# Tables of reciprocals with five rows for each head, and three read-backs in place of seven

## The chip, the core and the metric

The kernel runs on one core of a Trainium2 chip. Five engines work side by side: TensorE (PE in the profile, its weight loads PEld), VectorE (DVE), ScalarE (ACT), GpSimd (POOL) and SyncE (SP), which here only issues transfers. Sixteen DMA engines move data between DRAM and the on-chip memories. The metric is the device time of one execution in microseconds.

## What is computed

Two linear-attention blocks (A and B) work on the same input of 2048 tokens by 640 features and are mixed by a gate. Each has 32 heads of 20 features.

```python
q, k, v = qkv[0], qkv[1], qkv[2]
phi = lambda t: jnp.where(t > 0, t + 1, jnp.exp(t)) + 1e-6
pq, pk = phi(q), phi(k)
kv = jnp.einsum("bhsd,bhse->bhde", pk, v)
z = jnp.einsum("bhsd->bhd", pk)
num = jnp.einsum("bhqd,bhde->bhqe", pq, kv)
den = jnp.einsum("bhqd,bhd->bhq", pq, z)[..., None] + 1e-6
o = num / den
... @ wo
g = _sigmoid((x * gate_w).sum(-1, keepdims=True))
return g * a + (1 - g) * b
```

The division has one denominator for each head and token. It can be moved ahead: the query features `pq` of a head are multiplied by 1/den of that head before the last matmul.

## The kernel before

Everything is bf16 with f32 sums. `XT` holds the transposed input, `PK[X]` the key features of branch X by token (16 tiles of 128), `PQ[X]` the query features with features on the partitions: five tiles `k` of 128 features by 2048 tokens, worked in four blocks `b` of 512 tokens. Tiles 0 and 1 hold the even and the odd features of the first 256 in turn, tiles 2 and 3 those of the next 256, and tile 4 the last 128. So in the first pair partition p holds features of head p // 10, in the second those of head (128 + p) // 10, and in tile 4 that of head (512 + p) // 20.

The order of the engines' work is written out by hand: a list of operations, each with what it reads and writes, from which a small scheduler (`_Sched`) derives the semaphore waits. Each engine does its operations in the order of that list. A transfer is issued by SyncE in its own order, and its waits stand in SyncE's queue ahead of it, so a transfer whose data isn't ready holds up all that stand behind it.

The stages: keys of both branches (`k_tile`), queries (`q_tile`) with branch A's products `x^T pk` (`g_piece`) between them, then branch B's products, then for each branch the combined weights `WP` (`m_part`, `wp_tile`), and the final tiles: `fin_mm(X, t)` multiplies 128 tokens of `PQ[X]` with `WP[X]`; ScalarE scales branch A's by the gate (`fin_a`, line 793), VectorE adds branch B's (`fin_out`, line 805), and the tile is stored.

Around the change, all within `wp_a_den` (line 885), which is put on the list just after the second of branch B's 20 pieces: `den` (line 637) puts the denominators of one branch into one bank of 128 partitions, where partition 32 b + h holds head h of block b and the columns are the block's 512 tokens. VectorE adds the small constant (line 652) and takes reciprocals in four quarters of 128 columns (line 660) into `RC[X]`. `table(X)` (line 672) writes `RC[X]` to the DRAM tensor `rs[X]` of 32 rows (heads) by 2048 columns (tokens). `widen(X, b0, b1)` (line 682) reads it back into `RXW[X]`, where each partition has the reciprocals of its own head; there are three groups `i`, for the two pairs and for tile 4. Since 128 isn't a multiple of 10 or 20, a group begins or ends within a head, and the list `runs` (line 666) has seven transfers for the three groups: (group, first partition, first head, heads, partitions per head). Block 0 of A, block 0 of B, blocks 1 to 3 of A and blocks 1 to 3 of B are read back in this order, 28 transfers.

`scale(X, b)` (line 694) multiplies block b of `PQ[X]`: one VectorE instruction for the four tiles of the two pairs (line 699), one for tile 4 (line 707). On the list `scale("A", 0)` stands among branch B's products; `scale("B", 0)` behind final tiles A0 and A1, `scale("A", 1)` behind `WP` of branch B, just ahead of `fin_mm("A", 3)`, and the other five between output tiles. Tile t reads block t // 4: A4 is the first to need A's block 1.

`RXW["A"]` lies over the first ten tiles of `PK["A"]`, and `RXW["B"]` over three chunks of `XT`; the keys in `RX_LAP` stand for the memory that they share. All transfers go through `dma` (line 283), so a transfer is L291 in the profile, and all matmuls through `mms`, L302.

Of the kernel before, what the change touches and what calls it, by code (L numbers as in the profile page):

```python
# [7 lines left out]
dt = mybir.dt  # L8
# [3 lines left out]
S = 2048  # L12
D = 640
H = 32
DH = 20
NT = 16
NB = 4
# [188 lines left out]
def bass_gated_mix__linear_attn_block__linear_attn_block__prompt_kernel(  # L206
# [10 lines left out]
    consts = nc.inline_tensor(_build_consts(), name="kconsts")  # L217
    cap = consts.ap().bitcast(dt.bfloat16)

    rs = {X: nc.dram_tensor("rs" + X, [H, S], dt.bfloat16).ap() for X in ("A", "B")}  # L220
    wqkv = {"A": A_wqkv, "B": B_wqkv}
    wo = {"A": A_wo, "B": B_wo}
    BR = ("A", "B")
# [1 line left out]
    with ExitStack() as es:  # L225
        E = es.enter_context

        def sb(name, shape, dtype=dt.bfloat16):
            return E(nc.sbuf_tensor(name, shape, dtype))
# [16 lines left out]
        RXW = {  # L246
            "A": PK["A"][:, 0:10, :].rearrange("p t f -> p (t f)")[:, 0 : 3 * S].rearrange("p (i n) -> p i n", i=3),
            "B": XT[:, 0:3, :],
        }
        RX_LAP = {  # L250
            "A": [("PK", "A", t) for t in range(10)],
            "B": [("XT", t, c) for t in range(NT) for c in range(3)],
        }
# [12 lines left out]
        RC = {X: sb("RC" + X, [128, 512]) for X in BR}  # L266
# [16 lines left out]
        def dma(eng, name, o_ap, i_ap, reads=(), writes=(), transpose=False, noncontig=None):  # L283
            sem = new_sem(name)

            def fn(engobj):
                if noncontig is not None:
                    with nc.allow_non_contiguous_dma(reason=noncontig):
                        ins = engobj.dma_start(o_ap, i_ap, transpose=transpose)
                else:  # L290
                    ins = engobj.dma_start(o_ap, i_ap, transpose=transpose)  # L291
                return ins.then_inc(sem, 16)

            return sch.op(eng, fn, reads=reads, writes=writes, name=name, sem=sem, total=16)
# [19 lines left out]
        def dve(fn, reads=(), writes=(), name=""):  # L314
            return sch.op("DVE", fn, reads=reads, writes=writes, name=name)
# [33 lines left out]
        def load_wk(eng, X, c0, c1):  # L349
# [19 lines left out]
            reads=[("ONE",)],  # L369
            writes=[("IDN",)],  # L370
# [3 lines left out]
            writes=[("SGE", 0)],  # L374
# [7 lines left out]
        for b in range(1, NB):  # L382
            for c in range(NC):
# [5 lines left out]
                    writes=[("XT", t, c) for t in range(4 * b, 4 * b + 4)],  # L389
# [247 lines left out]
        def den(X, bk):  # L637
            xi = BR.index(X)
            steps = []
            for k in range(NC):  # L640
                for b in range(NB):
                    o = bank(bk, 0, 512, 32 * b, 32 * b + 32)
                    r = PQ[X][:, k, 512 * b : 512 * b + 512]
                    steps.append((o, ZBD[:, NC * xi + k, :], r, k == 0, k == NC - 1, (0, 32 * b)))
            mms(
                steps,
                reads=[("ZBD", X)] + [("PQ", X, b, k) for k in range(NC) for b in range(NB)],
                writes=[("PS", bk)],
                name="den%s" % X,
            )  # L650
            dve(
                lambda e: e.tensor_scalar(DT32[X][:, :], bank(bk, 0, 512), EPS, None, op0=ALU.add),  # L652
                reads=[("PS", bk)],
                writes=[("DT", X)],
            )

        def recip(X, i):
            def rcp(e):
                with nc.allow_low_precision(reason="r goes into a bf16 matmul"):
                    return e.reciprocal(RC[X][:, 128 * i : 128 * i + 128], DT32[X][:, 128 * i : 128 * i + 128])  # L660

            dve(rcp, reads=[("DT", X)], writes=[("RC", X, i)])

        runs = (
# [3 lines left out]
        )  # L670

        def table(X):
            dma(
                "SP",
                "rs" + X,
                rs[X].rearrange("h (b n) -> b h n", b=NB),
                RC[X][:, :],
                reads=[("RC", X, j) for j in range(4)],
                writes=[("RS", X)] + RX_LAP[X],
            )  # L680

        def widen(X, b0, b1):
            for n, (i, p0, h0, nh, m) in enumerate(runs):
                c0, c1 = 512 * b0, 512 * b1
                dma(
                    "SP",
                    "rx%s%d%d" % (X, b0, n),
                    RXW[X][p0 : p0 + nh * m, i, c0:c1],
                    rs[X][h0 : h0 + nh, c0:c1].unsqueeze(1).to_broadcast([nh, m, c1 - c0]),
                    reads=[("RS", X)],  # L690
                    writes=[("RX", X, i, p0, b) for b in range(b0, b1)],
                )

        def scale(X, b):
            cols = slice(512 * b, 512 * b + 512)
            pairs = RXW[X][:, 0:2, cols]
            v = PQ[X][:, 0:4, cols].rearrange("p (i a) n -> p i a n", i=2)
            dve(
                lambda e: e.tensor_tensor(
                    out=v, in0=v, in1=pairs.unsqueeze(2).to_broadcast([128, 2, 2, 512]), op=ALU.mult  # L700
                ),
                reads=[("RX", X) + r[0:2] + (b,) for r in runs if r[0] < 2] + RX_LAP[X],
                writes=[("PQ", X, b, k) for k in range(4)],
            )
            v4 = PQ[X][:, 4, cols]
            dve(
                lambda e: e.tensor_tensor(out=v4, in0=v4, in1=RXW[X][:, 2, cols], op=ALU.mult),  # L707
                reads=[("RX", X) + r[0:2] + (b,) for r in runs if r[0] == 2] + RX_LAP[X],
                writes=[("PQ", X, b, 4)],
            )  # L710

# [27 lines left out]
        def wp_tile(X, k, pp):  # L739
            P = PP[pp]  # L740
            cells = []
            for g in range(4):
                w = 8 + g // 2 if k == 4 else 4 * (k // 2) + g
                fs = slice(32 * (g % 2), 32 * (g % 2) + 32) if k == 4 else slice(k % 2, 64, 2)
                cells.append((w, MG[:, w, fs]))
            for j, (lo, hi) in enumerate(((0, D // 2), (D // 2, D))):
                mms(
                    [
                        (P[32 * g : 32 * g + 32, 512 * j : 512 * j + hi - lo], l, wo_at(X, w)[0][:, lo:hi], True, True, (0, 32 * g))
                        for g, (w, l) in enumerate(cells)  # L750
                    ],
                    reads=[("WO", X, w) for w, _ in cells] + [("MG", w) for w, _ in cells],
                    writes=[("PS", 2 * pp + j)],
                    name="wp%s%d" % (X, k),
                )
            for j, (lo, hi) in enumerate(((0, D // 2), (D // 2, D))):
                o, p = WP[X][:, k, lo:hi], P[:, 512 * j : 512 * j + hi - lo]
                (dve if j else act)(
                    lambda e, o=o, p=p, j=j: e.tensor_copy(o, p) if j else e.activation(o, p, ACT.Copy),
                    reads=[("PS", 2 * pp + j)],  # L760
                    writes=[("WP", X, k, j)],
                )
# [96 lines left out]
        for i in range(8):  # L859
            n = 3 * i + 9  # L860
# [24 lines left out]
        def wp_a_den():  # L885
            for k in range(NC):
                wp_tile("A", k, (1, 2, 3)[k % 3])
            den("A", 6)
            den("B", 7)
            for X in BR:  # L890
                for i in range(4):
                    recip(X, i)
                table(X)
            for b0, b1 in ((0, 1), (1, NB)):
                for X in BR:
                    widen(X, b0, b1)
# [4 lines left out]
            _Chain(nA, [(0, lambda: z_turn("B", 7))]),  # L901
            _Chain(nA, [(0, lambda: [m_part("A", 0, 8, 2), m_part("A", 8, NW, 3)])]),
            _Chain(nA + 1, [(0, wp_a_den), (15, lambda: scale("A", 0))]),
        ]
        _interleave(mains, chains)
        for t in (0, 1):
            fin_mm("A", t)
            fin_a(t)
        scale("B", 0)
        m_part("B", 0, 8, 7)  # L910
        m_part("B", 8, NW, 6)
        fin_mm("A", 2)
        for k in range(NC):
            wp_tile("B", k, (0, 3, 1)[k % 3])
        fin_a(2)
        scale("A", 1)
        fin_mm("A", 3)
        fin_a(3)
# [51 lines left out]
```

## Time and profile before

| | us |
|---|---|
| three runs | 194.4, 194.55, 196.41 |
| their median | 194.55 |
| the profiled execution | 195.57 |
| its span, first to last instruction | 193.8 |

| engine | busy us | share of the span |
|---|---|---|
| PE | 188.9 | 97% |
| DVE | 124.7 | 64% |
| ACT | 75.1 | 39% |
| POOL | 44.5 | 23% |

The page divides the span into 40 slices of 4.85 us; a digit is the busy share in tenths (9 is 90% or more), the last line the GB/s moved by all DMA engines:

```profile
PE   8999999999999999999999999999999799999994
DVE  0298999998995766767667645880334646482663
DMA  6994569983400000021000012002235631111213
GB/s 184 315 140 88 102 155 373 365 290 102 112 4 0 0 3 0 21 52 33 3 0 2 0 43 66 3 27 84 81 112 156 190 134 52 53 68 68 71 68 101
```

TensorE's row has one slice below 8 within the program, the 32nd, from 150 to 155 us. The DMA row shows the loads of the first 55 us, two later loads of weights, the tables and read-backs from 126 to 158 us, and the output behind them. In these views a name like `PKA<-rsA` is a transfer into the memory of `PK["A"]`, where `RXW["A"]` lies, and `XT<-rsB` one into `RXW["B"]`; a name in an issue row on SPq is the transfer issued, and its duration is that of the issue, not of the data's way.

### The profile page before, as it was taken

How to read it: one execution, taken by the hardware profiler on the slowest of the kernel's cores; microseconds unless marked ns; L12 is line 12 of the kernel's file. 1: busy time of each engine (PE TensorE's matmuls, PEld its weight loads, DVE VectorE, ACT ScalarE, POOL GpSimd, SP SyncE). 2: the span in 40 equal slices, each digit the busy share in tenths (PEclk: the TensorE clock that was granted, in tenths of full speed). 3: DMA queues.
4: the chain of work that ended last, by engine and by line, in shares of the span. 5: the costliest groups of instructions: out<-in, count | busy, mean ns of one | idle time of the engine just before them, and what ended most of it. 6: DMA issues, size and time to landing. Idle time of an engine off the chain costs nothing.

```text
span 193.8 us, 3584 instructions
## 1 busy us (share of the span) xinstructions
PE 188.9 (97%) x1428; PEld 103.6 (53%) x1428; DVE 124.7 (64%) x211; ACT 75.1 (39%) x130; POOL 44.5 (23%) x36
## 2 busy tenths in 40 slices
PE   8999999999999999999999999999999799999994
PEld 4555555555454544444544457555557355555552
DVE  0298999998995766767667645880334646482663
ACT  3366465655642624443425233111134332233301
POOL 1000223253226566637456500000000000000000
PEclk9999999999999999999999999999999999999999
DMA  6994569983400000021000012002235631111213
GB/s 184 315 140 88 102 155 373 365 290 102 112 4 0 0 3 0 21 52 33 3 0 2 0 43 66 3 27 84 81 112 156 190 134 52 53 68 68 71 68 101
DMA packets 20867, 18.02 MB, mean 93 GB/s; under 512 B 9265, under 2 KB 20082, under 8 KB 20850
## 3 DMA queue, kind: packets, MB, share of 16 engines
q1 hardware_dynamic: 20130, 17.05, 30.6%
q10 hardware_dynamic: 720, 0.74, 1.1%
q8 instruction: 11, 0.18, 0.4%
q14 instruction: 6, 0.05, 0.1%
HBM read 12.94 MB, written 2.88 MB: 82 GB/s over the span
## 4 chain that ended last, share of the span: by engine, by line
PE 80%; SPq 8%; DMA 5%; DVE 4%; issue 1%; ACT 0%; DVEq 0%; ACTq 0%
PE ps L302 79%; SPq L291 8%; DMA PKA<-rsA 4%; DVE RCA L660 2%; DVE RCB L660 2%; DMA XN<-in_A_x_dram 1%; PE ps L425 1%; ACT PKB L793 0%; DVE DTB L652 0%; DVE OSTG L805 0%; DVEq L940 0%; DVE PQA L707 0%; DVE XT L439 0%; ACTq L158 0%; DVEq L158 0%
## 5 line engine op out<-in xcount | busy, mean ns | idle before, releaser
L536 ACT ACTIVATE EQ<-ps 128x512 bf16<-128x512 f32 x40 | 23.9, 597 | 34.1 <-PE ps L302 34.0
L495 ACT ACTIVATE EK<-ps 128x640 bf16<-128x640 f32 x32 | 22.4, 703 | 16.3 <-PE ps L302 15.7
L541 DVE TENSOR_SCALAR EQ<-EQ 128x512 bf16<-128x512 bf16 x40 | 15.3, 382 | 17.9 <-ACT EQ L536 17.1
L302 PE MATMUL ps<-WPA,PQA 128*128 128x512 bf16 (+1 forms) x160 | 24.2, 299 | 1.3 <-DVE PQA L707 1.3
L588 POOL TENSOR_TENSOR ZS<-ZS,PKA 128x640 f32<-128x640 f32 x13 | 18.7, 1439 | 27.3 <-DVE PKB L511 12.1
L302 PE MATMUL ps<-PKA,XN 128*128 128x512 bf16 (+1 forms) x160 | 24.8, 299 | 0.0
L805 DVE SCALAR_TENSOR_TENSOR OSTG<-ps,SG,PKB 128x640 bf16<-128x640 f32 (+1 forms) x17 | 14.2, 843 | 16.0 <-PE ps L302 14.7
L793 ACT ACTIVATE PKB<-ps,SG 128x640 f32<-128x640 f32 x16 | 12.7, 795 | 30.4 <-PE ps L302 30.4
L302 PE MATMUL ps<-WPB,PQB 128*128 128x512 bf16 (+2 forms) x160 | 23.9, 299 | 0.0
L302 PE MATMUL ps<-WKA,XT 128*128 128x512 bf16 (+1 forms) x160 | 23.2, 299 | 0.1
L302 PE MATMUL ps<-XT,WQB 128*128 128x512 bf16 x100 | 23.2, 379 | 0.0
L302 PE MATMUL ps<-XT,WQA 128*128 128x512 bf16 x100 | 23.1, 379 | 0.0
L302 PE MATMUL ps<-WKB,XT 128*128 128x512 bf16 (+1 forms) x160 | 22.5, 299 | 0.0
L302 PE MATMUL ps<-PKB,XN 128*128 128x512 bf16 (+1 forms) x160 | 22.2, 299 | 0.0
L588 POOL TENSOR_TENSOR ZS<-ZS,PKB 128x640 f32<-128x640 f32 x13 | 19.1, 1470 | 13.5 <-DVE PQB L546 11.0
L302 PEld LDWEIGHTS ps<-PKA,XN 128*128 128x128 bf16 x160 | 13.1, 98 | 11.7
L302 PEld LDWEIGHTS ps<-WPA,PQA 128*128 128x128 bf16 x160 | 12.8, 98 | 11.1 <-DVE PQA L707 1.4
L302 PEld LDWEIGHTS ps<-WPB,PQB 128*128 128x128 bf16 x160 | 13.0, 98 | 9.2
L302 PEld LDWEIGHTS ps<-WKB,XT 128*128 128x128 bf16 x160 | 12.4, 97 | 9.6
L302 PEld LDWEIGHTS ps<-WKA,XT 128*128 128x128 bf16 x160 | 12.3, 98 | 9.6 <-DVE XT L439 0.8
L302 PEld LDWEIGHTS ps<-PKB,XN 128*128 128x128 bf16 x160 | 12.2, 98 | 9.6 <-issue 0.4
L506 DVE TENSOR_SCALAR EK<-EK 128x640 bf16<-128x640 bf16 x32 | 14.6, 457 | 2.1 <-ACT EK L495 1.9
(64 smaller groups left out, 155.5 us busy)
## 6 DMA issues: line engine op xcount, KB each, us to landing
out_dram<-OSTG SPq DMA_DIRECT2D x15, 160.0 KB, 1.8
XN<-in_A_x_dram SPq DMA_DIRECT2D x3, 640.0 KB, 9.0
PKA<-rsA SPq DMA_DIRECT2D x3, 360.0 KB
XT<-rsB SPq DMA_DIRECT2D x3, 360.0 KB
WKB<-in_B_wqkv_dram SPq DMA_DIRECT2D x1, 800.0 KB, 6.8
WQA<-in_A_wqkv_dram SPq DMA_DIRECT2D x1, 800.0 KB, 5.3
WVA<-in_A_wqkv_dram SPq DMA_DIRECT2D x1, 800.0 KB, 11.4
WQB<-in_B_wqkv_dram SPq DMA_DIRECT2D x1, 800.0 KB, 12.4
```

Of the source, the lines that this page charges most:

```text
L291: ins = engobj.dma_start(o_ap, i_ap, transpose=transpose)
L302: ins = pe.matmul(o, l, r, start=st, stop=sp, tile_position=tp)
L425: ins = pe.transpose(dst[:, 128 * i : 128 * i + 128], XN[:, t, 128 * c : 128 * c + 128], IDN[:, :],)
L495: lambda e: e.activation(EK[:, slot, :], P[:, 0:D], ACT.Exp),
L506: lambda e: e.tensor_scalar(EK[:, slot, :], EK[:, slot, :], 1.0, EPS, op0=ALU.min, op1=ALU.add),
L536: lambda e: e.activation(EQ[:, slot, :], bank(bk, 0, 512), ACT.Exp),
L541: lambda e: e.tensor_scalar(EQ[:, slot, :], EQ[:, slot, :], 1.0, EPS, op0=ALU.min, op1=ALU.add),
L588: lambda e: e.tensor_tensor(out=o, in0=a, in1=PK[X][:, t, :], op=ALU.add),
L660: return e.reciprocal(RC[X][:, 128 * i : 128 * i + 128], DT32[X][:, 128 * i : 128 * i + 128])
L793: lambda e: e.activation(TA[:, t % 5, :], PP[pp][:, 0:D], ACT.Copy, scale=SG[:, 0, t : t + 1]),
L805: lambda e, lo=lo, hi=hi, at=at: e.scalar_tensor_tensor(out=OSTG[:, slot, lo:hi], in0=PP[pp][:, at : at + hi - lo], scalar=SG[:, 1, t : t ...
```

## The change

The DRAM tables get five rows for each head instead of one: 160 rows by 2048 columns. A table is written in four transfers, one for each block of 512 tokens; each reads the 32 partitions of its block five times over. With five rows for each head, row r of the table belongs to head r // 5, and each group of 128 partitions is a whole number of rows: 64 rows twice, the next 64 rows twice, the last 32 rows four times. So `maps` takes the place of `runs`, and a group is read back by one transfer of 128 partitions. The four read-backs are on the list in the same order as before, each now of three transfers; each waits for the table blocks that it reads, not for a whole table.

```diff
-    rs = {X: nc.dram_tensor("rs" + X, [H, S], dt.bfloat16).ap() for X in ("A", "B")}
+    rs = {X: nc.dram_tensor("rs" + X, [5 * H, S], dt.bfloat16).ap() for X in ("A", "B")}
...
-        runs = (
-            (0, 0, 0, 12, 10), (0, 120, 12, 1, 8),
-            (1, 0, 12, 1, 2), (1, 2, 13, 12, 10), (1, 122, 25, 1, 6),
-            (2, 0, 25, 1, 8), (2, 8, 26, 6, 20),
-        )
-
-        def table(X):
+        maps = ((0, 64), (64, 64), (128, 32))
+
+        def table(X, b):
             dma(
                 "SP",
-                "rs" + X,
-                rs[X].rearrange("h (b n) -> b h n", b=NB),
-                RC[X][:, :],
+                "rs%s%d" % (X, b),
+                rs[X][:, 512 * b : 512 * b + 512].rearrange("(h r) n -> h r n", r=5),
+                RC[X][32 * b : 32 * b + 32, :].unsqueeze(1).to_broadcast([32, 5, 512]),
                 reads=[("RC", X, j) for j in range(4)],
-                writes=[("RS", X)] + RX_LAP[X],
+                writes=[("RS", X, b)] + (RX_LAP[X] if b == 0 else []),
             )
 
         def widen(X, b0, b1):
-            for n, (i, p0, h0, nh, m) in enumerate(runs):
-                c0, c1 = 512 * b0, 512 * b1
+            c0, c1 = 512 * b0, 512 * b1
+            for i, (g0, n) in enumerate(maps):
                 dma(
                     "SP",
-                    "rx%s%d%d" % (X, b0, n),
-                    RXW[X][p0 : p0 + nh * m, i, c0:c1],
-                    rs[X][h0 : h0 + nh, c0:c1].unsqueeze(1).to_broadcast([nh, m, c1 - c0]),
-                    reads=[("RS", X)],
-                    writes=[("RX", X, i, p0, b) for b in range(b0, b1)],
+                    "rx%s%d%d" % (X, b0, i),
+                    RXW[X][:, i, c0:c1],
+                    rs[X][g0 : g0 + n, c0:c1].unsqueeze(1).to_broadcast([n, 128 // n, c1 - c0]),
+                    reads=[("RS", X, b) for b in range(b0, b1)],
+                    writes=[("RX", X, i, b) for b in range(b0, b1)],
                 )
...
             for X in BR:
                 for i in range(4):
                     recip(X, i)
-                table(X)
+                for b in range(NB):
+                    table(X, b)
             for b0, b1 in ((0, 1), (1, NB)):
                 for X in BR:
                     widen(X, b0, b1)
```

In `scale` only the keys of what is read change with it; the order of VectorE, ScalarE, GpSimd and TensorE is the same. The lines behind `scale` move up by four in the new file, so line 699 becomes 695, 707 becomes 703, and 805 becomes 801.

More of the change, by code (lines that the diff above doesn't have):

```diff
@@ L701, in scale @@
                 ),
-                reads=[("RX", X) + r[0:2] + (b,) for r in runs if r[0] < 2] + RX_LAP[X],
+                reads=[("RX", X, i, b) for i in (0, 1)] + RX_LAP[X],
                 writes=[("PQ", X, b, k) for k in range(4)],
@@ L707, in scale @@
                 lambda e: e.tensor_tensor(out=v4, in0=v4, in1=RXW[X][:, 2, cols], op=ALU.mult),
-                reads=[("RX", X) + r[0:2] + (b,) for r in runs if r[0] == 2] + RX_LAP[X],
+                reads=[("RX", X, 2, b)] + RX_LAP[X],
                 writes=[("PQ", X, b, 4)],
```

## The prediction

> **What bounds the kernel now.** I read the page's engine shares first, then TensorE's own waits, then the chain of waits, then the order of TensorE, VectorE and SyncE's queue around the one gap. TensorE is busy for 188.9 of the 193.8 us, at a granted clock of 1.00, so only about 5 us of the span can be had from any change that leaves the matmuls alone. TensorE's waits say who holds it up (engine and line, who released it, total us, times, longest):
>
> ```profile
> PE ps L302 <- DVE PQA L707: 1.3, 1, 1.3
> PE ps L302 <- PEq L955: 0.8, 1, 0.8
> ```
>
> The second is the start of the program. The first is the only wait within it: one matmul group waits for the multiplication of line 707, the second instruction of `scale`. The chain that ended last (start, us, what) says what lies behind it:
>
> ```profile
> 126.91 3.26 DVE RCB L660 x4
> 130.17 0.02 issue
> 130.18 0.52 SPq L291
> 130.70 0.05 issue
> 130.75 0.85 SPq L291
> ...
> 145.39 0.64 SPq L291
> 146.03 0.04 issue
> 146.07 7.67 DMA PKA<-rsA
> ...
> 153.83 0.44 DVE PQA L707
> 154.27 0.05 issue
> 154.31 35.51 PE ps L302 x260
> ```
>
> Read from the top: B's reciprocals, B's table, then 21 transfers issued one after another by SyncE (A's block 0, B's block 0, A's blocks 1 to 3), the last landing 7.67 us after its issue began, the multiplication, and then 35.5 us of matmuls without a gap. The gap itself, in the order of time of TensorE and then VectorE:
>
> ```profile
> 151.53 1.52 PE L302 MATMUL ps<-WPB,PQB 128*128 128x512 bf16 x10
> 154.31 1.53 PE L302 MATMUL ps<-WPA,PQA 128*128 128x512 bf16 x10 [1.27 <-DVE PQA L707]
> 155.68 1.52 PE L302 MATMUL ps<-WPB,PQB 128*128 128x512 bf16 x10
> ```
>
> ```profile
> 138.62 0.43 DVE L707 TENSOR_TENSOR PQA<-PQA,PKA 128x512 bf16<-128x512 bf16 x1 [0.60 <-DMA PKA<-rsA]
> 150.96 1.21 DVE L699 TENSOR_TENSOR PQA<-PQA,PKA 128x2048 bf16<-128x2048 bf16 x1
> 153.83 0.42 DVE L707 TENSOR_TENSOR PQA<-PQA,PKA 128x512 bf16<-128x512 bf16 x1 [1.66 <-DMA PKA<-rsA]
> ```
>
> Final tile A4 (`fin_mm("A", 4)`) starts at 154.31 because the fifth multiplication of A's block 1 stood 1.66 us waiting for its reciprocals. Block 0 is not late: its last multiplication ends at 139.05 and tile A0 starts at 142.38, behind branch B's products, so 3.3 us are spare there.
>
> **Cost of the table writes.** The table of A is issued at 126.94; its packets move in a stretch of 1.7 us (window, us, the busy times of PE, PEld, DVE, ACT and POOL, clock, share of the 16 DMA engines, GB/s), and for comparison the output stores between 158.5 and 164 us, in 40 slices:
>
> ```profile
> 128.30:130.00 1.70, 1.70 (x15) 0.97 (x13) 1.70 (x3) 0.41 (x1) 0.00 (x0) 1.00 0.25 75
> ```
>
> ```profile
> DMA  0000599700000000000000018993500000000000
> GB/s 22 19 19 28 186 382 354 261 19 0 0 0 0 0 0 0 0 0 0 0 0 0 0 65 317 354 345 103 129 0 0 0 0 0 0 0 0 0 0 0
> ```
>
> A share of 0.25 is what four engines give when they never rest: 1.7 x 75 GB/s is the table's 128 KB, some 19 GB/s for each. An output store of 128 rows fills the engines (nine tenths) and moves at 317 to 382 GB/s. The diff makes each table block 32 heads outermost, where the old table had 4 blocks outermost. By the nearer row in shape (a store from many partitions, 1,280 B rows) a new block of 160 rows, 164 KB, takes 0.5 us; by the old table's rate 2.2 us. I take 0.5; the other end is the second rival. [...]
>
> **Cost of the issues.** SyncE's queue goes from 2 + 28 issues to 8 + 12. One issue of an uneven transfer takes 0.58 to 0.86 us (median 0.70) in the rows now, the two tables 0.67 and 0.52; the even ones (80 rows of `wo`, 128 rows of output) 0.31 to 0.43. The new ones are all even, so I take 0.4, with 0.85 as the upper end; 0.05 lies between two. A's four blocks are issued from 126.94 to 128.7 while VectorE still makes B's reciprocals, which end at 130.17; they cost nothing at 0.4, and at 0.85 push B's to 130.5. B's four: 130.2 to 132.0 (upper end 134.1). A's three for block 0: to 133.3 (136.8). B's three: to 134.7 (139.5). A's last three: to 136.0 (142.2), now 146.8. B's last three: to 137.4 (144.9), now 152.0. The first output store is issued at 155.08, so nothing queued behind these on SyncE is held up at either end.
>
> **Added waits.** Each read-back now waits for the semaphores of its own blocks. Stores land 1.6 to 4.5 us after issue (output, median 1.8). A's block 0 is issued at 126.94, so it has landed by 131.4 at the latest, and its reader is not due before 132.0; B's block 0 has 133.3 - 130.2 = 3.1 us, enough by the median, 1.4 short at the worst, which would push back only transfers that have 4 us or more to spare (below). So I cost the waits at nothing.
>
> **When block 0 of A is ready.** Now its last multiplication starts 138.62 - 135.99 = 2.6 us after the end of the last of its seven issues. The same lag after 133.3 gives 135.9, and 139.4 at the upper end; plus 0.43. Tile A0 needs it by 142.38. No loss at either end; the issue price would have to pass 1.26 us per table for one (126.94 + 8 x 1.26 + 3 x 0.75 = 139.3, plus 2.6).
>
> **When block 1 of A is ready.** Before it has to come block 0 of both branches, 0.79 MB, and A's three blocks, 1.18 MB. Between 142 and 154 us the windows now show 131 to 225 GB/s for the same packets. From 132.5 that gives 141 to 148 us, without counting that the load becomes more even. At the slow end of the issues, 142.2 plus the 7.67 us of today's last landing is 150. Either way before VectorE comes to it: it finishes B's weight copies at 151.0, and the first multiplication starts at 150.96 as now. In every later pair without a wait the second starts 1.17 us after the first (158.12 and 159.29), so it starts at 152.13, and 0.48 us after that (154.31 - 153.83) tile A4 could start: 152.61.
>
> **What is late next.** TensorE itself. Tiles follow each other every 1.36 us (155.68, 157.04), so A4 starts at 151.53 + 1.36 = 152.89, with 0.28 us of spare. Gain: 154.31 - 152.89 = 1.42 us; the idle time of 1.27 is the lower bound. Everything behind moves with it: the next multiplications follow output tiles on VectorE, and the tightest, B's block 1, ends at 159.7 for a tile at 163.8.
> TensorE's own pace doesn't depend on the transfers: ScalarE's five evacuations of branch B's products come every 4.34 or 4.35 us from 125.25 to 142.63, whether the DMA share of the window is 0 or 0.44. So earlier transfers neither slow nor help it.
>
> **Sum.** The profiled execution took 195.57 us (span 193.8 and 1.8 around it); 195.57 - 1.42 = 194.15. The three runs have a median of 194.55, 1.0 below the profiled one, and the matmuls behind the gap are the same: 194.55 - 1.42 = 193.1, or 0.7% less.
>
> **Rivals.**
> First, the stall goes but the gain isn't kept, or the reciprocals still come as late: 194.5. For it: the spare behind A4 is only 0.28 us, so a slower weight copy or multiplication gives back the same amount, and the transfers would have to stay 8 us late to keep the wait. Against it: all of the 28 issues that make the chain are cut to 12. Chance 0.12.
> Second, slower: the block writes stay at 75 GB/s, since rows repeated five times from 32 partitions are in no row of this trace. Eight blocks at 2.2 us from 128.3 end at 145.8; the read-back of A's block 0 stands behind them, and with its 2.6 us the last multiplication starts at 148.4 instead of before 141.9, so tile A0 waits 6.5 us, less the 1.42: 199.6. It decides once the blocks end after about 139, that is below 1.31 MB / 10.7 us = 122 GB/s. Against it: the output stores at over 300 GB/s. Chance 0.14, milder forms included.
> Third, faster than that: the wait that goes is longer in runs without a profile (one of the three took 196.41), as a landing of 7.67 us is the least steady piece of the chain. A gain of 2.2 us would give 192.3. Chance 0.10.
> The forecast has the remaining 0.64.
>
> **How the numbers follow.** A run of this kernel can tell about 1% from no change. The forecast is 193.1, and by itself 192.5 to 193.5 with the two bounds of the gap and the spread of the two closest runs (194.4 and 194.55) taken twice over. Faster by over 1% is under 192.6: the third rival and 0.02 of the forecast's edge, 0.12. Slower by over 1% is over 196.5: 0.12 of the second rival. Within 1%: 0.62 of the forecast, the first rival's 0.12 and 0.02 of mild forms of the second, 0.76. The range takes in the forecast, the first rival, those mild forms and the near edge of the third: 192.4 to 195.0.
>
> **What would show it.** Right: TensorE without a wait for line 703 (707's new place), the table writes at a DMA share well over 0.25, 20 issues of about 0.4 us, the last before 145 us, and VectorE's wait for transfers only before block 0. Wrong: a wait of TensorE before tile A0 near 142 us (second rival), or a new gap near 153 (first).

## The result, and the profile after

| | before | changed |
|---|---|---|
| timed runs | 20 | 20 |
| median, us | 195.44 | 194.34 |
| lowest and highest, us | 194.09, 196.82 | 194.01, 194.88 |
| the profiled execution, us | 195.57 | 194.69 |
| its span, us | 193.8 | 192.9 |

The ratio of the times is 0.9948, with a 95% interval of 0.9924 to 0.9972: the changed kernel is half a per cent faster. The row of extremes says more than the medians. Both kernels have the same lowest time within 0.1 us; what went is the upper half of the old times. Of the 20 runs of the kernel before, 9 were below 194.9 us and 11 above 195; the three times shown ahead of the prediction were two of the low kind and one of the high.

First TensorE's waits in the changed kernel (engine and line, who released it, total us, times, longest):

```profile
PE ps L302 <- PEq L952: 0.8, 1, 0.8
PE ps L425 <- DMA XN<-in_A_x_dram: 0.2, 1, 0.2
PE ps L302 <- ACT WPB L755: 0.2, 1, 0.2
PE ps L302 <- issue: 0.2, 1, 0.2
```

The wait for the fifth multiplication, 1.3 us before, is gone. The first two lines belong to the start of the program. The last two are most likely no idle time: the page of the profile lists 1402 matmuls beside 1428 weight loads, so 26 records are missing, and each gap of 0.16 us stands at a stretch that lacks records (9 of 10 in the group at 150.94 us). The page's summary of the chain that ended last has no SyncE queue and no reciprocals left in it:

```profile
PE 94%; DMA 1%; ACT 1%; issue 1%; DVE 0%; DVEq 0%; ACTq 0%
```

The same stretch in the order of time, TensorE and then VectorE (start, us):

```profile
152.08 1.52 PE L302 MATMUL ps<-WPB,PQB 128*128 128x512 bf16 x10
153.44 1.52 PE L302 MATMUL ps<-WPA,PQA 128*128 128x512 bf16 x10
154.79 1.52 PE L302 MATMUL ps<-WPB,PQB 128*128 128x512 bf16 x10
```

```profile
138.35 1.23 DVE L695 TENSOR_TENSOR PQA<-PQA,PKA 128x2048 bf16<-128x2048 bf16 x1 [7.64 <-DMA PKA<-rsA]
139.50 0.42 DVE L703 TENSOR_TENSOR PQA<-PQA,PKA 128x512 bf16<-128x512 bf16 x1
...
151.51 1.22 DVE L695 TENSOR_TENSOR PQA<-PQA,PKA 128x2048 bf16<-128x2048 bf16 x1
152.65 0.42 DVE L703 TENSOR_TENSOR PQA<-PQA,PKA 128x512 bf16<-128x512 bf16 x1
```

Tile A4 follows at the pace of 1.36 us, and the fifth multiplication of block 1 starts 1.14 us after the first, waiting for nothing. Block 0, on the other hand, comes no sooner than before in this execution (138.35 for 136.79). SyncE's queue and then the windows of the table writes and of the read-backs (PE, PEld, DVE, ACT, POOL, clock, share of the DMA engines, GB/s) show why:

```profile
127.49 2.63 SPq L291 DMA_DIRECT2D rsA<-RCA  x4
130.74 2.49 SPq L291 DMA_DIRECT2D rsB<-RCB  x4
133.28 1.92 SPq L291 DMA_DIRECT2D PKA<-rsA  x3
135.24 2.82 SPq L291 DMA_DIRECT2D XT<-rsB  x3
138.60 1.81 SPq L291 DMA_DIRECT2D PKA<-rsA  x3
140.53 1.83 SPq L291 DMA_DIRECT2D XT<-rsB  x3
```

```profile
131.00:133.00 2.00, 2.00 (x17) 1.15 (x16) 0.00 (x0) 0.00 (x0) 0.00 (x0) 1.00 0.78 199
143.00:145.00 2.00, 1.95 (x15) 1.06 (x14) 0.00 (x0) 1.16 (x2) 0.00 (x0) 1.00 0.85 270
```

An issue takes 0.6 us, not 0.4, and the eight table blocks move at some 200 GB/s at a share near 0.8 (199 and 0.78 from 131 to 133 us), where the old table had 0.25: 164 KB in 0.8 us each. The block-0 read-backs stand behind them. Blocks 1 to 3 then flow at 270 GB/s at a share of 0.85. In the kernel before, the share was 0.49 while the same blocks were on their way:

```profile
148.00:150.00 2.00, 2.00 (x47) 1.25 (x44) 1.04 (x3) 1.18 (x4) 0.00 (x0) 1.00 0.49 131
```

**Where the time went, in three pieces.** Tile A0 starts at some time, A4 some time after it, and the execution ends some time after that. In the two profiled executions:

| execution | time | A0 starts | A0 to A4 | rest |
|---|---|---|---|---|
| before | 195.57 | 142.38 | 11.93 | 41.26 |
| changed | 194.69 | 142.93 | 10.51 | 41.25 |

Rest is the time less the start of A4. The middle piece is 11.93 - 10.51 = 1.42 us shorter, just the gap that the prediction priced, and 0.55 of it doesn't show because this execution reached A0 later. It was that much behind already at the start: in the chains of the two, the long stretch of matmuls begins at 8.37 us before and at 8.92 us here. Of this, 0.12 us is the first transfer of `XN` (landed at 3.57 and 3.69 us), the rest the first matmuls behind it; the change touches neither.

### The profile page after: what moved, and what is told of

It is laid out like the page before. It is cut to its first block, busy times and chain, and to the rows that moved or that the text cites. A ratio compares the mean times of both kernels' runs of the same rounds, so it can differ in the third digit from the quotient of the medians.

```text
span 192.9 us, 3543 instructions
## 1 busy us (share of the span) xinstructions
PE 187.7 (97%) x1402; PEld 104.0 (54%) x1428; DVE 124.5 (65%) x211; ACT 75.2 (39%) x130; POOL 44.5 (23%) x36
## 4 chain that ended last, share of the span: by engine, by line
PE 94%; DMA 1%; ACT 1%; issue 1%; DVE 0%; DVEq 0%; ACTq 0%
PE ps L302 93%; DMA XN<-in_A_x_dram 1%; PE ps L425 1%; ACT WPB L755 1%; ACT PKB L789 0%; DVE OSTG L801 0%; DVEq L937 0%; ACTq L158 0%
## 5 line engine op out<-in xcount | busy, mean ns | idle before, releaser
L302 PE MATMUL ps<-WPA,PQA 128*128 128x128 bf16 (+1 forms) x155 | 23.3, 296 | 0.4 <-ACT WPB L755 0.2
L302 PE MATMUL ps<-WPB,PQB 128*128 128x128 bf16 (+2 forms) x157 | 23.4, 297 | 0.2
L302 PE MATMUL ps<-WKB,XT 128*128 128x129 bf16 (+1 forms) x157 | 22.3, 297 | 0.2
L302 PE MATMUL ps<-PKB,XN 128*128 128x512 bf16 (+1 forms) x156 | 21.7, 297 | 0.3 <-issue 0.2
```

Of the source, the lines that this page charges most:

```text
L302: ins = pe.matmul(o, l, r, start=st, stop=sp, tile_position=tp)
```

## Experiments

Two theories of the old wait were put against each other. S: the seven old read-backs loaded some of the 16 DMA engines much more than others, so the last ones finished late. N: 28 issues, one after another on SyncE, were too many. A third, V, is about the times: that the wait differs from execution to execution, and makes the spread of the old kernel.

**The kernel before, profiled twice more** (no edit).

> The kernel before, unchanged, one more profiled execution. Theory V (the wait of TensorE before tile A4 differs from execution to execution and makes the spread of 194.1 to 196.8 us): the time less the excess of the distance from tile A0 to tile A4 over 10.5 us lies between 194.0 and 194.9, whatever the time is; a time below 194.9 goes with no wait. Rival (the spread comes from elsewhere, the start for instance): the wait is near 1.3 us again while the time differs.

> The kernel before, unchanged, a third profiled execution: the same two expectations as for the second. Theory V: time less wait between 194.0 and 194.9. Rival: a wait near 1.3 us in each.

TensorE's wait at A4 in the first, and the same two tiles in the second:

```profile
154.93 1.53 PE L302 MATMUL ps<-WPA,PQA 128*128 128x512 bf16 x10 [1.57 <-DVE PQA L707]
```

```profile
151.87 1.52 PE L302 MATMUL ps<-WPB,PQB 128*128 128x512 bf16 x10
153.22 1.52 PE L302 MATMUL ps<-WPA,PQA 128*128 128x512 bf16 x10
```

| execution | time | A0 starts | A0 to A4 | rest |
|---|---|---|---|---|
| before, second profile | 196.16 | 142.69 | 12.24 | 41.23 |
| before, third profile | 194.47 | 142.72 | 10.50 | 41.25 |

The same program has a wait of 1.57 us in one execution and none in the other, with SyncE's issues at the same times within 0.03 us (A's blocks 1 to 3 at 141.98 and 142.01). Time less the excess over 10.5 is 194.4 and 194.5, as V expected. So the lower edge of the old times is the kernel without its wait. That the wait makes the whole spread is shown for these three executions; of the other runs only the times are known.

**Seven read-backs again, but even ones** (from the changed kernel).

```diff
-        maps = ((0, 64), (64, 64), (128, 32))
+        maps = (
+            (0, 0, 64, 0, 32), (0, 64, 32, 32, 16), (0, 96, 32, 48, 16),
+            (1, 0, 64, 64, 32), (1, 64, 64, 96, 32),
+            (2, 0, 64, 128, 16), (2, 64, 64, 144, 16),
+        )
...
-                    RXW[X][:, i, c0:c1],
-                    rs[X][g0 : g0 + n, c0:c1].unsqueeze(1).to_broadcast([n, 128 // n, c1 - c0]),
+                    RXW[X][p0 : p0 + m, i, c0:c1],
+                    rs[X][g0 : g0 + n, c0:c1].unsqueeze(1).to_broadcast([n, m // n, c1 - c0]),
```

There are 28 read-backs, seven in the place of each three, of 32 or 64 partitions and of 16 or 32 rows each.

> [...] Theory S (the old read-backs were late because they loaded a few of the 16 engines more than the rest): no wait of TensorE before tile A4 or at most 0.2 us, A0 to A4 10.5 us, times of 194.0 to 194.9 as for the changed kernel. Theory N (28 issues one after another on SyncE were the cause): a wait of about 1.3 us in the profile, times spread up to 196 as for the kernel before.

12 runs from 193.93 to 194.80, where the kernel before on the same chip went from 194.05 to 196.48 (23 runs); ratio 0.997 (0.9943 to 0.9997). A0 to A4 took 10.51 us. SyncE is as busy as in the kernel before:

```profile
142.64 4.35 SPq L291 DMA_DIRECT2D PKA<-rsA  x7
```

These seven are issued from 142.64 to 146.99; the old ones from 141.67 to 146.80. The wait is gone with 28 issues as late as before, so N, the theory that the number of issues was the cause, falls. The share of the DMA engines is higher with the even cut: 0.68, 0.85 and 1.06 in the three windows of 2 us from 144 to 150, where the kernel before has 0.54, 0.50 and 0.49.

**Old tables, three read-backs.** The tables of the kernel before, written in two transfers, are read back by three transfers of 128 partitions, each from 16 rows; of the edit the list of read-backs is shown.

```diff
-        maps = ((0, 64), (64, 64), (128, 32))
+        maps = ((0, 16), (8, 16), (16, 16))
```

> The old tables of 32 rows (two transfers) with three read-backs of 128 partitions, each of 16 rows read by 8 partitions; the rows aren't those of the right heads, so the reciprocals are other heads'. Theory S (even loading of the engines is all that matters): no wait before A4, A0 to A4 10.5 us, 194.0 to 194.9. Theory H (many partitions reading the same DRAM row is what made the old read-backs slow, and the five copies cured it): a wait of 1 us or more remains, times up to 196.

12 runs from 193.98 to 194.88, ratio 0.996 (0.9934 to 0.9987), A0 to A4 10.51 us. Eight partitions read each row, and nothing is late, so five copies don't help by themselves. They let 128 partitions be cut into whole rows of the right heads. H, the theory that many readers of one row made the old read-backs slow, is not yet refuted by this run alone, because the old ones had 10 and 20 readers for a row; the kernel with four rows for each read-back, below, has 32. The writing of the copies costs something elsewhere: here block 0's first multiplication starts at 135.52, in the two profiles of the changed kernel at 138.35 and 136.53.

**One transfer of the seven made more even** (from the kernel before).

```diff
-            (2, 0, 25, 1, 8), (2, 8, 26, 6, 20),
+            (2, 0, 25, 1, 8), (2, 8, 14, 12, 10),
```

> The kernel before with one entry of its list changed: the last transfer of a group, 120 partitions from 6 heads, reads 12 heads for 10 partitions each instead (so tile 4 is multiplied by the reciprocals of other heads). Issues and bytes stay. [...] Theory N (issues): no difference, ratio 1.000, times up to 196.5.

12 runs from 194.03 to 194.81; the kernel before on this chip from 193.86 to 196.13 (17 runs); ratio 0.998 (0.9958 to 1.0002). The interval just touches 1, but the upper tail is gone, and the profile has no wait at A4, with SyncE as before (A's seven from 142.16, lasting 5.17 us):

```profile
151.40 1.22 DVE L699 TENSOR_TENSOR PQA<-PQA,PKA 128x2048 bf16<-128x2048 bf16 x1
152.53 0.42 DVE L707 TENSOR_TENSOR PQA<-PQA,PKA 128x512 bf16<-128x512 bf16 x1
```

One profile alone wouldn't prove it, since one profile in three of the kernel before has no wait either; the times do more: none of 12 above 194.81, where 7 of 17 were above 195.

**Read-backs of four rows** (from the changed kernel).

```diff
-                    rs[X][g0 : g0 + n, c0:c1].unsqueeze(1).to_broadcast([n, 128 // n, c1 - c0]),
+                    rs[X][g0 : g0 + 4, c0:c1].unsqueeze(1).to_broadcast([4, 32, c1 - c0]),
```

> The changed kernel with each read-back taking 4 rows for 32 partitions each, so that the outermost dimension is 4 (the reciprocals are those of other heads). Theory S: 4 of 16 engines at some 75 GB/s move 1.97 MB in 26 us from 134.5, so A's blocks 1 to 3 land near 160 and TensorE waits about 8 us before A4: 202 to 203. Theory N (only the number of issues counts): no wait, 194.3.

201.87 us. The windows show a DMA share of 0.26 while TensorE stands (first row):

```profile
153.00:157.50 4.50, 0.05 (x1) 0.00 (x0) 1.68 (x3) 0.00 (x0) 0.00 (x0) 1.00 0.26 100
157.50:160.00 2.50, 2.47 (x11) 1.30 (x12) 0.77 (x1) 0.05 (x1) 0.00 (x0) 0.62 0.40 152
```

The time is just below the 202 to 203 that S gave, in two parts. A0 to A4 took 15.15 us, 4.6 more than it needs, not 8, as packets of 3 KB moved at 100 GB/s rather than 75. The rest was 44.34 instead of 41.2: a second wait of 1.1 us, and matmuls at a granted clock of 0.62 behind the first one. The number of issues and the bytes are those of the changed kernel; what was changed is the outermost count, and with it the share fell to 0.26, from 0.85 in the changed kernel. It costs some 7.5 us. The edit also lets 32 partitions read each row, but that isn't what slows it: as an estimate from the shares, 100 GB/s at 0.26 of 16 engines is 24 GB/s for each busy engine, and the changed kernel's 270 GB/s at 0.85 is 20. So H falls too.

**The tables alone, block by block** (from the kernel before).

```diff
-        def table(X):
+        def table(X, b):
...
-                rs[X].rearrange("h (b n) -> b h n", b=NB),
-                RC[X][:, :],
+                rs[X][:, 512 * b : 512 * b + 512],
+                RC[X][32 * b : 32 * b + 32, :],
```

> The kernel before with its tables of 32 rows written block by block (four transfers for each branch), the seven read-backs unchanged. Theory S: no gain, as the read-backs are as uneven as before; three more issues for B at 0.6 us push the read-backs back by 1.8 us, so the wait before A4 grows to about 3 us: 196 to 198. Theory P (writing and waiting block by block is what brings the gain): no wait, 194.3.

There is no gain, so P, the theory that writing and waiting block by block helps, falls. Eight runs went from 194.59 to 196.49 us, with a ratio of 1.0038 (1.0006 to 1.0071); two more took 198.48 and 199.06 and are not in the ratio. Seven of the eight are above 195, where 7 of 23 were of the kernel before on this chip, and four of the eight reach the 196 at S's lower end. So the wait, as far as the times tell, shows in nearly every run instead of in some.

The read-backs of A's blocks 1 to 3 are issued later than before: the last issue ends at 148.58 for 146.80, and 1.3 of the 1.8 us remain when each is counted from the start of B's first table issue. The one trace kept is of the fastest run, 194.59, which has no wait of TensorE: the fifth multiplication started at 152.89 (153.83, 154.44 and 152.71 in the three profiles of the kernel before), and A0 to A4 took 10.52 us. It doesn't show what happened in the runs that took longer.

**One table of five rows for each branch** (from the changed kernel).

```diff
-                rs[X][:, 512 * b : 512 * b + 512].rearrange("(h r) n -> h r n", r=5),
-                RC[X][32 * b : 32 * b + 32, :].unsqueeze(1).to_broadcast([32, 5, 512]),
+                rs[X].rearrange("(h r) (b n) -> b h r n", r=5, b=NB),
+                RC[X][:, :].unsqueeze(1).to_broadcast([128, 5, 512]),
```

> The changed kernel with each branch's five-row table in one transfer, blocks outermost as in the kernel before. If the outermost count of 4 limits it to four engines (the old table's 75 GB/s): 655 KB in 8.7 us, B's behind A's until about 146, the read-back of A's block 0 caught behind it, tile A0 about 6 us late: about 200. If the table spreads over all engines: no wait, 194.3.

200.94 us. Blocks outermost bring back the share of a quarter (0.26 at 80 GB/s, columns as above), and A0 waits behind it:

```profile
129.00:136.00 7.00, 6.95 (x54) 3.93 (x53) 1.54 (x2) 1.41 (x2) 0.00 (x0) 1.00 0.26 80
```

```profile
147.71 2.85 PE L302 MATMUL ps<-WPA,PQA 128*128 128x512 bf16 x10 [4.79 <-DVE PQA L703]
```

This is the course of the second rival, with its place right. The changed kernel writes the same rows in four transfers for each branch with a block's 32 heads outermost, and its writes had a share of 0.78.

**The changed kernel again** (no edit).

> The changed kernel, unchanged, against the kernel before on this chip. Theory V: its times lie within about 0.9 us (194.0 to 194.9), those of the kernel before reach from the same lower end to above 196; ratio of 0.993 to 0.998. Rival: the lowest times of the two differ by more than 0.5 us.

12 runs from 193.96 to 194.92, the kernel before from 194.17 to 196.55 (23 runs): the lower ends are 0.21 us apart, as V says. Its profiled execution (194.17) has no wait either: A0 starts at 142.43, A0 to A4 takes 10.50 us, and the rest 41.24. The ratio is 0.998 (0.9957 to 1.0004). It is nearer to 1 than the first time because on this chip 16 of 23 runs of the kernel before were below 194.9, against 9 of 20 in the first comparison. How often the wait shows differs from one set of runs to the next.

## Why the prediction was right about the wait and wrong in the sum

**Right.** The old kernel's one wait is that for blocks 1 to 3 of A, it goes whole, and nothing takes its place: TensorE is late next, at its own pace of 1.36 us for a tile. For the execution that was profiled the 1.42 us were exact: 11.93 to 10.51 us from A0 to A4. Tile A0 isn't made late by the tables, and TensorE's pace didn't change: the rest is 41.23 to 41.26 us in the five profiled executions of the two kernels.

**Wrong: the sum for the median.** The step was "The three runs have a median of 194.55, 1.0 below the profiled one, and the matmuls behind the gap are the same: 194.55 - 1.42 = 193.1". The wait of the profiled execution was taken off a time that hardly held it. The profiled execution came out at 195.57 - 1.42 = 194.15 without its wait, and that was the answer: the changed kernel's median is 194.34, and no run of it went under 193.96. Measured from the 194.55 that the sum started with, the gain is 0.2 us and not 1.4. The runs of 194.4 and 194.55 lay within 0.4 us of 194.15; the one of 196.41 lay 2.3 above. The clue was in the prediction's own words: a difference of 1.0 between median and profile, nearly the size of the wait, was passed over as an offset of the profile. The third rival named the right thing (a wait that differs from run to run, with 196.41 as its sign) and drew the wrong end from it: a variable wait means that removing it cuts off the upper times, not that the lower ones move. The table of pieces makes it plain: time is start of A0 (142.3 to 142.9) plus 10.5 plus wait plus 41.2, and only the wait can be taken away: 0 to 1.7 us in the three profiles. The slowest runs, at up to 196.82, had some 2 us, as an estimate, if their other pieces were the same; they left no trace. The same subtraction from the median of all 20 runs, 195.44, would have given 194.0, but by luck: a median holds the wait or not according to how many runs have it.

**Sizes that were off and cost nothing.** A table block of 164 KB was put at 0.5 us from the output stores; it took 0.8 (about 200 GB/s). An issue was put at 0.4 us because the new transfers are even. No run shows that for a read-back: the twelve of the changed kernel took 0.51 to 0.62 us and one of them 1.53, at a median of 0.60, for 0.70 with the uneven cut. A table block's issue took 0.6, and a plain block of 32 rows, in the kernel with the tables alone, 0.42 (1.70 us for four). Together they made the last multiplication of A's block 0 start at 139.50 instead of 135.9, a little past the upper end of 139.4, and still 3.0 us ahead of A0 (139.92 to 142.93). In the second profile of the changed kernel it started at 138.31. The price of 2.2 us for a block at the old table's rate, the second rival's end, was wrong for the changed kernel, but that rate came in the kernel that keeps the blocks outermost (80 GB/s). A0 waited 4.79 us there, where the rival had 6.5. That its 200.94 still came out above the rival's 199.6 goes with a slower TensorE clock behind the wait (0.50, the last section), which the rival didn't have.

**Evenness, not the number of transfers.** The prediction priced the issues, and left the evener load out of its times, and no trace shows the load of each engine. It said that all 28 issues make the chain, where the chain that it shows has the 21 up to A's last. But earlier issues aren't what the wait needs in order to go. Even transfers with 28 issues remove the wait, evening out one of the seven removes it, and three transfers of four rows each make it longer than any other (4.48 us). Late issues do matter where the cut is uneven: in the kernel with the tables alone, issued 1.3 us later than before, seven of the eight times in the ratio are above 195. Even read-backs issued nearly as late (142.64, for 143.41 there) have none above 194.80. Few transfers with the old uneven cut weren't tried, so whether earlier issues alone would have been enough isn't shown.

What the runs show of the cut is its share of the DMA engines: 0.25 to 0.26 with an outermost count of 4 (the old table, the one table for each branch, the read-backs of four rows), 0.78 for the writes with 32 outermost, 0.49 to 0.54 from 144 to 150 us for the old read-backs with 12, 1, 1, 12, 1, 1 and 6 heads outermost, 0.68 to 1.06 there for the even seven. The trace doesn't say which engine carried which packet. So S, as a theory of how many rows each engine had, isn't shown. What is shown is that no profile has the wait with 16 to 64 rows outermost in each read-back, and none with 12 in the place of the 6.

**Left open.** What makes the old wait come in one execution and not in the next. Of the 768 read-back packets of 3 KB, with a median of 0.12 us in both, 12 took more than 0.6 us in the first profile of the kernel before (up to 1.44, from 147.6 to 151.9 us) and 12 in the changed kernel (up to 1.94, from 142.2 to 143.8), where nothing was late for them. Whether the wait comes when such a stretch meets the last rows of an uneven read-back wasn't tried.

## What to carry to other kernels

Before a wait is taken off a time, see whether that time holds it: a stall on a transfer can be there in one execution and absent in the next (1.57 us and none here), so take it off the execution that shows it, and see whether the lowest times are the kernel without it. When a transfer lands late, look at the share of the DMA engines while it is due. Here it was 0.49 to 0.54 in the profile with the wait of 1.27 us and 0.26 in the one of 4.48 us, with transfers queued (but 0.55 and 0.45 from 146 to 150 us in the third profile of the kernel before, without a wait), and what helped was another cut of the transfers (their outermost count), with as many of them. Copies in DRAM that make the cut even cost little here, where the writes lie in a stage with time to spare: block 0 was ready later (its first multiplication at 138.35 and 136.53 for 135.52 without copies), but still ahead of A0.

## What the runs showed of the hardware

After a wait of 4.79 us in the kernel with one table for each branch, the granted clock of TensorE fell to 0.50:

```profile
147.70:149.00 1.30, 1.29 (x4) 0.47 (x5) 0.37 (x1) 0.00 (x0) 0.00 (x0) 0.50 0.76 203
149.00:150.70 1.70, 1.56 (x8) 0.96 (x8) 1.19 (x2) 0.04 (x1) 0.00 (x0) 0.50 0.97 327
150.70:152.00 1.30, 1.22 (x11) 0.74 (x11) 0.00 (x0) 0.75 (x1) 0.00 (x0) 0.96 1.03 293
```

It stood at 0.50 for some 3 us (147.7 to 150.7) and at 0.96 in the next window. Without the wait A0 would have started at 142.92, so 0.54 us had been lost ahead of it. The 5.33 us by which A0 came late (147.71 for 142.38 in the kernel before), 0.54 and 4.79, were followed by 1.5 more (A0 to A4 in 12.01 us, not 10.51), and they add up to the 6.8 between its 200.94 and the 194.10 of the execution with seven even read-backs, whose A0 started at 142.37. Behind the wait of 4.48 us in the kernel with read-backs of four rows the clock was 0.62 from 157.5 to 162 us, and 1.00 after that. The old kernel's gap of 1.27 us left it at 1.00. So the wait of 4.79 us cost some 1.5 us more than its own time, and the one of 1.27 us nothing.
